# Decode attention and gated MLP on one core: V loads on GpSimd's queue, K loads on SyncE's

## The chip, the cores and the metric

The kernel runs on one core of one Trainium2 chip. The time is device microseconds of one execution; three runs of the kernel before gave 1279.21, 1279.48 and 1279.5 us, median 1279.48 us. Lower is better.

## The reference

One decode step of a transformer layer: layer norm, attention over a cached K and V, a residual, a second layer norm and a sigmoid-gated MLP with a residual. Batch B is 4, one query position, model width 512, 32 heads of 128, a cache of 8192 positions, MLP width 1792, all in bf16.

```python
def _A_ref(x, k_cache, v_cache, wq, wo):
    q = (x @ wq).reshape(B, Sq, H, Dh).transpose(0, 2, 1, 3)
    scores = einsum("bhqd,bhkd->bhqk", q, k_cache) * Dh ** -0.5
    o = einsum("bhqk,bhkd->bhqd", softmax(scores, axis=-1), v_cache)
    return o.transpose(0, 2, 1, 3).reshape(B, Sq, H * Dh) @ wo
def _B_ref(x, w_gate, w_up, w_down):
    return (sigmoid(x @ w_gate) * (x @ w_up)) @ w_down
h  = x + _A_ref(layernorm(x), k_cache, v_cache, wq, wo)
h2 = h + _B_ref(layernorm(h), w_gate, w_up, w_down)
```

k_cache and v_cache have 4 x 32 x 8192 x 128 values each, 268 MB apiece; the weights together are about 14 MB.

## The kernel before

**Units and slots.** The work is cut into NU = 32 units of HU = 4 heads each. The K of a unit, and its V, is one load of 128 partitions x 64 KB, 8 MB. SBUF has three such slots in the tile KV: K alternates between slots 0 and 1, V always uses slot 2, except the last V, which goes to slot 0. Slot 2 first holds wq, so V of unit 0 waits until the q projection (L300, token `t_qp`) has read it. After the last unit, wo, w_gate and w_up go to slot 1 and w_down to slot 2.

**One unit** (`unit`, L421). `scores(u)`: 16 chunks; for each, VectorE transposes 128 x 1024 words of K into one of two halves of kT (L334) and TensorE multiplies it with q in four matmuls (L343). `maxima(u)`: a small memset on VectorE (L360) gives the token `t_kd[u]`, "K of unit u has been read", then come the maximum (L361 to L366) and the exponential on ScalarE (L368). Then `pv(u - 1)`, the product with V of the unit before: 64 matmuls on TensorE (L404), which wait for the load of V, a scaled copy on ScalarE (L409), and a gathering matmul (L414), of which the first one gives `t_vd[u-1]`, "V of unit u-1 has been read". Then `weights(u)`: VectorE transposes the exponentials (L374), and TensorE sums them (L378). L374 waits for the L414 matmuls of the unit before, since the tile PTz is used again. The three compute engines run these in program order; each engine has its own list of instructions, and `_Prog` puts in the waits.

**Loads.** All big loads stand on SyncE's queue in one written order (`order`, L224; issued at L540): k0, k1, v0, k2, v1, k3, and so on to k31, v30, v31. K of unit u waits for `t_kd[u-2]`, V of unit u for `t_vd[u-1]`, the last V for `t_kd[30]`. SyncE issues in order, so a load whose wait is over still stands behind the one ahead of it. Then come 40 empty instructions, and wo (L545), w_gate (L547), w_up (L551), which wait for `t_kd[31]`, and w_down in three pieces (L556), which wait for `t_vd[30]`.

**Semaphores.** A load counts 16 on the semaphore of its slot: k0, k1 and v2 belong to one waiting engine each ("private"), which counts them down again in its loop (`_rebase`); the last V counts on v0.

**The end.** After the last unit TensorE runs filler matmuls (L387) and the last product with V, then the output projection (L474), the layer norm, the gated MLP (L491 to L520) and the output.

**GpSimd** makes masks, identities and zeros in the first 8 us and then does nothing.

Of the kernel before, what the change touches and what calls it, by code (L numbers as in the profile page):

```python
# [18 lines left out]
class _Prog:  # L19
# [52 lines left out]
    def emit(self, eng, fn, waits=(), incs=1, ch=None):  # L72
        todo = self._waits(eng, waits)
        key = ch or eng
        tok = self.token(key, incs) if incs else None
        self._put(eng, todo, key, fn, incs, 1)
        return tok
# [41 lines left out]
def bass_sequential_preLN__mha_block_cached__glu_gated_glu__decode_kernel(  # L119
# [20 lines left out]
    NU = B * H // HU  # L140
    R = S // 32
    SLOT = R * DH
# [11 lines left out]
    prog = _Prog({"p2d": "dve", "d2d": "dve", "a2d": "dve", "d2p": "pe", "a2p": "pe",  # L154
                  "d2a": "act", "p2a": "act",
                  "k0": "dve", "k1": "dve", "v2": "pe"})
    emit = prog.emit

    with ExitStack() as es:
# [39 lines left out]
        def reg(slot, off, size):  # L199
            return KV[:, slot * SLOT + off:slot * SLOT + off + size]  # L200
# [14 lines left out]
        bank = [PS[:, 512 * i:512 * (i + 1)] for i in range(8)]  # L215
        SBK, OBK, EX, XS, XO, QB, DN = 0, 1, 2, 3, 4, (5, 6), 7

        keys = ["sp", "act", "dve", "pool", "pe", "p2x", "d2x", "x", "pad", "out0", "wq", "wg", "v0", "v1"]
        keys += [f"wd{i}" for i in range(len(WDT) - 1)] + [f"wu{i}" for i in range(len(WUC) - 1)] + ["wo"]
        keys += list(prog.private)  # L220
        for k in keys:
            prog.sems[k] = es.enter_context(nc.semaphore("s_" + k))

        order = [("k", 0)] + [x for u in range(1, NU) for x in (("k", u), ("v", u - 1))] + [("v", NU - 1)]  # L224
        slots = {(x, u): (0 if u == NU - 1 else 2) if x == "v" else u % 2 for x, u in order}
        toks = {x: prog.token(x[0] + str(slots[x]), 16) for x in order}
        t_wq = prog.token("wq", 16)
        t_wo = prog.token("wo", 16)
        t_wg = prog.token("wg", 16)
# [64 lines left out]
        for g in range(2):  # L294
# [8 lines left out]
            t_qp = emit("pe", f, [t_wq, t_xn, t_ps0, t_selc], incs=4)  # L303

            src = bank[QB[g]].rearrange("p (k w r) -> p r k w", k=8, r=2)
# [6 lines left out]
        t_tr, t_sc, t_pv, t_ex, t_mx, t_exp, t_ptz, t_lq, t_ocp, t_rs, t_kd, t_vd, t_sum = ({} for _ in range(13))  # L312
# [125 lines left out]
        for u in range(1, NU):  # L438
            t, first = divmod(u - 1, TU)
            if u == NU - 1:  # L440
                prog.close("dve", "act")
                t = 0
# [81 lines left out]
        for t in range(NFT):  # L524
            if t == 0:
# [4 lines left out]

        prog.dma("sp", "wq", lambda e: e.dma_start(reg(2, 0, NC * H * DH), A_wq.rearrange("(p c) f -> p (c f)", p=128)),
                 tok=t_wq)
        for n, (x, u) in enumerate(order):
            w = t_qp if n == 2 else None
            if n >= 3:
                w = t_kd[u - 2] if x == "k" else t_kd[NU - 2] if u == NU - 1 else t_vd[u - 1]
            slot = slots[x, u]
            cache = A_v_cache if x == "v" else A_k_cache
            src = cache[u // (NU // B), HU * (u % (NU // B)):HU * (u % (NU // B) + 1), :, :].rearrange("h (p r) d -> (h p) (r d)", p=32)
            prog.dma("sp", f"{x}{slot}", lambda e, src=src, slot=slot: e.dma_start(reg(slot, 0, SLOT), src), [w],  # L540
                     tok=toks[x, u])
        for _ in range(40):
            emit("sp", lambda e: e.nop(), ch="pad")
        k_done, v_done = t_kd[NU - 1], t_vd[NU - 2]
# [46 lines left out]
```

## Time and profile before

| | |
|---|---|
| time, median of three runs | 1279.48 us |
| lowest and highest | 1279.21 and 1279.5 us |
| span of the profiled execution, first to last instruction | 1277.7 us |
| TensorE matmul busy | 797.8 us (62%) |
| TensorE weight load busy | 327.1 us (26%) |
| VectorE busy | 763.3 us (60%) |
| ScalarE busy | 58.9 us (5%) |
| GpSimd busy | 5.7 us |
| moved by the DMA engines | 550.83 MB, mean 431 GB/s |
| mean granted TensorE clock | 0.822 |

The profiled execution has no time listed apart from its span; the runs listed beside it are some 1.8 us longer than the span, which starts at the first and ends at the last instruction.

How to read it: the span is cut into 40 slices of 31.9 us for the rows of busy tenths. In the groups and the timeline, a row is line, engine, operation, output<-input and count; in the timeline the first two numbers are the start and the length in us, and the bracket at the end is how long the engine had been idle and what released it. In the list of waits the three numbers are the us in total, the times and the longest. In the table of stretches each engine has its busy us and count, followed by the granted clock, the busy share of the 16 DMA engines and GB/s. Queue rows of the DMA part are packets, MB and the share of 16 engines' time. Rows of DMA issues end with the median us from issue to landing. SPq is SyncE's queue, ACTq ScalarE's.

### The profile page before, as it was taken

What the parts mean: (1) busy time and instruction counts of PE and PEld (TensorE: products, weight loads), DVE (VectorE), ACT (ScalarE), POOL (GpSimd) and SP (SyncE); (2) the same over time, 40 slices, a digit from 0 to 9 for tenths busy, and PEclk for the clock granted to TensorE, in tenths of its full rate; (3) what the DMA queues carried; (4) which work ended last, traced back from release to release, by engine and by line L of the source; (5) the groups of instructions that cost most, each with busy time, mean ns of one, the idle gap of its engine ahead of it and who ended that gap; (6) DMA issues with size and microseconds to landing.
All of it is one profiled execution on the core that took longest, in us unless ns stands there. A gap on an engine that the chain in (4) does not pass through costs nothing. (4 is left out here: it accounts for less than half of the span.)

```text
span 1277.7 us, 14121 instructions
## 1 busy us (share of the span) xinstructions
PE 797.8 (62%) x4636; PEld 327.1 (26%) x4636; DVE 763.3 (60%) x917; ACT 58.9 (5%) x114; POOL 5.7 (0%) x22
## 2 busy tenths in 40 slices
PE   1676765557755557655567655567555576555578
PEld 0232222222222223222222222222222232222233
DVE  1876665556665557665567655566655566655571
ACT  2000000000000000000000000000000000000001
POOL 1000000000000000000000000000000000000000
PEclk9988877788877788877788777788777888777888
DMA  9999999999999999999999999999999999999998
GB/s 427 427 425 429 427 455 427 431 427 435 447 427 431 427 437 445 427 431 427 445 437 429 429 427 451 431 429 429 427 453 429 429 429 427 455 427 429 429 429 368
DMA packets 10244, 550.83 MB, mean 431 GB/s; under 512 B 1144, under 2 KB 1152, under 8 KB 1408
## 3 DMA queue, kind: packets, MB, share of 16 engines
q1 hardware_dynamic: 10224, 550.77, 99.7%
q8 instruction: 2, 0.03, 0.0%
q14 instruction: 2, 0.02, 0.0%
q10 hardware_dynamic: 16, 0.01, 0.0%
HBM read 550.77 MB, written 0.00 MB: 431 GB/s over the span
## 5 line engine op out<-in xcount | busy, mean ns | idle before, releaser
L334 DVE STREAM_TRANSPOSE kT<-KV 128x1024 f32<-128x1024 f32 x512 | 615.1, 1233 | 301.1 <-DMA KV<-in_A_k_cache_dram 241.0
L343 PE MATMUL PS<-kT,Lq 128*128 128x512 bf16 x2048 | 586.1, 417 | 320.2 <-DVE kT L334 302.6
L343 PEld LDWEIGHTS PS<-kT,Lq 128*128 x2048 | 209.6, 102 | 697.0 <-issue 623.6
L374 DVE STREAM_TRANSPOSE PTz<-E_sb 32x512 bf16<-32x512 bf16 x128 | 89.9, 703 | 128.9 <-PE PS L414 125.2
L404 PE MATMUL PS<-KV,PTz 128*16 128x512 bf16 x2048 | 116.9, 381 | 0.0
L378 PE MATMUL PS<-part,headw 128*128 128x2 f32 x64 | 18.7, 362 | 100.5 <-DVE PTz L374 100.5
L368 ACT ACTIVATE E_sb<-PS,negm 128x512 bf16<-128x512 f32 x32 | 22.0, 687 | 1141.2 <-DVE negm L366 1141.2
L404 PEld LDWEIGHTS PS<-KV,PTz 128*16 128x16 bf16 x2048 | 58.3, 109 | 56.8 <-issue 13.2
L414 PE MATMUL PS<-lane,kT 128*128 128x4 f32 x256 | 33.6, 255 | 30.9 <-ACT kT L409 30.9
L361 DVE TENSOR_REDUCE part<-PS 128x1 f32<-128x512 f32 x32 | 22.1, 692 | 38.8 <-PE PS L343 38.8
L414 PEld LDWEIGHTS PS<-lane,kT 128*128 128x128 f32 x256 | 31.0, 191 | 46.3 <-issue 44.9
L378 PEld LDWEIGHTS PS<-part,headw 128*128 128x128 f32 x64 | 16.0, 310 | 103.7 <-DVE PTz L374 103.7
L321 PE MATMUL PS<-Lq,headw 128*128 128x512 bf16 x32 | 18.7, 585 | 10.9 <-issue 9.5
L409 ACT ACTIVATE kT<-PS,rsb 128x512 f32<-128x512 f32 x32 | 22.0, 687 | 61.1 <-PE PS L404 61.1
L387 PE MATMUL PS<-Lq 128*128 128x512 bf16 x44 | 13.7, 478 | 0.2 <-issue 0.2
L327 DVE TENSOR_TENSOR Lq<-q_all,mask 128x32 bf16<-128x32 bf16 x32 | 9.7, 303 | 0.0
L453 DVE TENSOR_TENSOR kT<-PS,mask 128x512 bf16<-128x512 f32 x1 | 0.7, 692 | 12.9 <-PE PS L414 12.9
L366 DVE STREAM_TRANSPOSE negm<-mxr 128x32 f32<-128x32 f32 x32 | 6.8, 212 | 1.1
L363 DVE STREAM_TRANSPOSE turn<-part 128x32 f32<-128x32 f32 x32 | 6.8, 212 | 1.1
L387 PEld LDWEIGHTS PS<-Lq 128*128 128x128 bf16 x44 | 4.8, 115 | 8.2 <-issue 5.8
L395 DVE RECIPROCAL rsb<-PS 128x1 f32<-128x1 f32 x32 | 6.5, 202 | 0.7 <-PE PS L378 0.7
L300 PE MATMUL PS<-KV,kT 128*4 128x512 bf16 x32 | 3.6, 627 | 5.1 <-DMA KV<-in_A_wq_dram 5.1
(70 smaller groups left out, 59.5 us busy)
## 6 DMA issues: line engine op xcount, KB each, us to landing
KV<-in_A_wq_dram SPq DMA_DIRECT2D x1, 4096.0 KB, 12.2
KV<-in_A_wo_dram SPq DMA_DIRECT2D x1, 4096.0 KB, 27.5
KV<-in_B_w_gate_dram SPq DMA_DIRECT2D x1, 1792.0 KB, 31.4
KV<-in_B_w_up_dram SPq DMA_DIRECT2D x1, 1792.0 KB, 35.2
KV<-in_B_w_down_dram SPq DMA_DIRECT2D x1, 1024.0 KB, 32.5
KV<-in_A_k_cache_dram SPq DMA_DIRECT2D x32, 49.8
KV<-in_A_v_cache_dram SPq DMA_DIRECT2D x32, 30.8
KV<-in_B_w_down_dram SPq DMA_DIRECT2D x1, 512.0 KB, 33.3
```

The lines of the kernel that those rows point to most:

```text
L321: emit("pe", lambda e: e.matmul(bank[bk], headb, zeros, start=True, stop=False, skip_group_check=True), waits, incs=0)
L327: t_lq[u] = emit("dve", lambda e, ix: e.tensor_tensor(dst, bass.AP(raw(q_all), at(ix, 0) * (4 * TU) + 4 * (u - TU * t), [[NU * 4, 128], [1 ...
L334: t_tr[u, c] = emit("dve", lambda e: e.transpose(kT[:, (c % 2) * TW:(c % 2 + 1) * TW], KVw[:, o:o + TW]), w, ch="d2p")
L343: ins = e.matmul(bank[SBK], bass.AP(raw(Lq), ix[-1] * 2 + (128 * t + c % 2), [[528, 128], [1, 128]]), rhs, start=False, stop=False, skip_g ...
L361: a = emit("dve", lambda e: e.tensor_reduce(part[:, 0:1], bank[SBK], AX.X, ALU.max), [t_sc[u, NT - 1], t_pool], ch="d2d")
L368: t_exp[u] = emit("act", lambda e: e.activation(E_sb[:, :], bank[SBK], ACT.Exp, bias=negm[:, 0:1], scale=SCALE, accum_out=part[:, 1:2]), [ ...
L374: return [e.transpose(PTz[32 * q:32 * (q + 1), :].rearrange("p (r q c) -> p r q c", r=4, q=4)[:, :, q, :], E_sb[32 * q:32 * (q + 1), :].re ...
L378: t_sum[u] = emit("pe", lambda e: e.matmul(bank[QB[1]][:, 0:2], headw[:, :], part[:, 0:2], start=True, stop=True), [t_ptz[u], t_selc], ch= ...
L387: emit("pe", lambda e: [e.matmul(bank[XS], Lq[:, 0:128], Lq[:, 0:512], start=True, stop=True) for _ in range(n)][-1], [t_ps0, t_lq[NU - 1] ...
L404: made.append(e.matmul(PS[32 * j:32 * j + 16, ob:ob + 512], lhsT, KV[:, slot * SLOT + 512 * k:slot * SLOT + 512 * (k + 1)], start=(k < 4), ...
L409: t_ocp[u] = emit("act", lambda e: e.activation(O_sb, bank[OBK], ACT.Copy, scale=rsb[:, 0:1]), [t_pv[u], t_rs[u]], ch="a2p")
L414: ins = e.matmul(bass.AP(raw(PS), at(ix, 0) * 4 + (512 * EX + 4 * (u - t)), [[4096, 128], [1, 4]]), O_sb[:, 128 * q:128 * (q + 1)], lane[: ...
```

## The change

V of units 0 to 28 is issued from GpSimd instead of SyncE, each with the same wait as before. Such a load counts on a new semaphore `vs`; GpSimd waits for it and then adds 16 to v2, on which TensorE waits, with an empty instruction. SyncE issues K of all 32 units, each with the same wait as before, then V of unit 29, the first half (by columns) of the last V, V of unit 30, and the second half of the last V; then the 40 empty instructions and the weights as before. The last V counts 32 on v0, for both halves. Slots and sizes are the same; the compute engines' code is not touched.

```diff
-        keys = ["sp", "act", "dve", "pool", "pe", "p2x", "d2x", "x", "pad", "out0", "wq", "wg", "v0", "v1"]
+        keys = ["sp", "act", "dve", "pool", "pe", "p2x", "d2x", "x", "pad", "vs", "out0", "wq", "wg", "v0", "v1"]
...
-        order = [("k", 0)] + [x for u in range(1, NU) for x in (("k", u), ("v", u - 1))] + [("v", NU - 1)]
+        order = [(x, u) for u in range(NU) for x in "kv"]
         slots = {(x, u): (0 if u == NU - 1 else 2) if x == "v" else u % 2 for x, u in order}
-        toks = {x: prog.token(x[0] + str(slots[x]), 16) for x in order}
+        toks = {x: prog.token(x[0] + str(slots[x]), 16 + 16 * (x == ("v", NU - 1))) for x in order}
+        APART = NU - 3
...
-        for n, (x, u) in enumerate(order):
-            w = t_qp if n == 2 else None
-            if n >= 3:
-                w = t_kd[u - 2] if x == "k" else t_kd[NU - 2] if u == NU - 1 else t_vd[u - 1]
+        def load(eng, x, u, w, a=0, b=SLOT):
             slot = slots[x, u]
             cache = A_v_cache if x == "v" else A_k_cache
             src = cache[...]
-            prog.dma("sp", f"{x}{slot}", lambda e, src=src, slot=slot: e.dma_start(reg(slot, 0, SLOT), src), [w],
-                     tok=toks[x, u])
+            if eng == "pool":
+                t = prog.dma(eng, "vs", lambda e: e.dma_start(reg(slot, a, b - a), src[:, a:b]), [w])
+                prog.dma(eng, f"{x}{slot}", lambda e: e.nop(), [t], tok=toks[x, u])
+            else:
+                prog.dma(eng, f"{x}{slot}", lambda e: e.dma_start(reg(slot, a, b - a), src[:, a:b]), [w], tok=toks[x, u])
+
+        for u in range(NU):
+            load("sp", "k", u, t_kd[u - 2] if u > 1 else None)
+        for u in range(APART):
+            load("pool", "v", u, t_vd[u - 1] if u else t_qp)
+        load("sp", "v", NU - 3, t_vd[NU - 4])
+        load("sp", "v", NU - 1, t_kd[NU - 2], 0, SLOT // 2)
+        load("sp", "v", NU - 2, t_vd[NU - 3])
+        load("sp", "v", NU - 1, t_kd[NU - 2], SLOT // 2)
```

## The prediction

> **What bounds the kernel now.** I read the page's queue table first, then the stretches of the span, then what SyncE's queue waited for, then single transfers in the timeline.
>
> ```profile
> span 1277.7 us, 14121 instructions
> PE 797.8 (62%) x4636; PEld 327.1 (26%) x4636; DVE 763.3 (60%) x917; ACT 58.9 (5%) x114; POOL 5.7 (0%) x22
> q1 hardware_dynamic: 10224, 550.77, 99.7%
> 90.60:1235.00 1144.40, 717.69 (x4094) 295.01 (x4094) 702.86 (x830) 42.48 (x87) 0.00 (x0) 0.81 1.00 433
> SPq L540 <- PE PS L414: 1124.4, 30, 38.5
> DVE kT L334 <- DMA KV<-in_A_k_cache_dram: 241.0, 31, 14.3
> ```
>
> No compute engine is busy for more than 62% of the span. The one queue that carries all bulk data, q1 (SyncE's), keeps the 16 DMA engines at work for 99.7% of it, and in the 1144 us stretch without start and end the DMA share is 1.00. The queue still waits 1124.4 us for L414, the matmul that frees V's only slot. That wait costs nothing, because a K load is always in flight beneath it. VectorE idles 241.0 us for K. So the bound is the sum of bytes: what the change can save is DMA idle time, of which 0.3% of 1277.7 = 3.8 us exist, and what it can cost is any moment in which no queue holds a load.
>
> The time of one load (8 MB, K or V), and the rest of the unit's schedule:
>
> ```profile
> 1175.23 2.37 DVE L334 STREAM_TRANSPOSE kT<-KV 128x1024 f32<-128x1024 f32 x2 [7.30 <-DMA KV<-in_A_k_cache_dram]
> 1196.48 0.06 DVE L360 MEMSET dumm<- 128x1 f32 x1
> 1197.64 3.65 PE L404 MATMUL PS<-KV,PTz 128*16 128x512 bf16 x64
> 1202.68 0.80 SPq L540 DMA_DIRECT2D KV<-in_A_v_cache_dram  x2
> 1203.42 2.90 DVE L374 STREAM_TRANSPOSE PTz<-E_sb 32x512 bf16<-32x512 bf16 x4 [4.04 <-PE PS L414]
> 1213.92 2.37 DVE L334 STREAM_TRANSPOSE kT<-KV 128x1024 f32<-128x1024 f32 x2 [7.60 <-DMA KV<-in_A_k_cache_dram]
> ```
>
> The first and last of these are the arrivals of K30 and K31 with one V between them: 38.69 us for two loads, **19.35 us per load**. K30 is scored (L334 transposes, L343 matmuls) from 1175.23 to the marker L360 at 1196.48, 21.2 us. TensorE starts the V product 1.16 us after that marker; 5.04 us after its start the V slot is free (the L540 issue at 1202.68), and 8.68 us after its start VectorE has finished the L374 transposes (1203.42 + 2.90) and can start the next K.
>
> The listed runs have a median of 1279.48 us; the span is 1277.7, so about 1.8 us lie around it. I make the sum against 1279.5. Less than 0.2% (2.6 us) would hardly be told from no change here.
>
> **The change, part by part.** *Removed:* SyncE's fixed order V(u), K(u+2). Before, both go out together when the V slot comes free, and are served one after the other. *Added:* V of units 0 to 28 on GpSimd's queue, and a semaphore step by GpSimd behind each. K(u+2) now leaves as soon as unit u is scored, some 6.2 us sooner (1202.68 less 1196.48). The bytes are the same, so nothing is gained while a load is always in flight.
>
> How two queues with bulk loads share the DMA engines is not in this trace. Its nearest rows are the small instruction queues in a stretch where q1 is full:
>
> ```profile
> q1 hardware_dynamic: 236, 13.50, 104.2%
> q8 instruction: 1, 0.02, 0.2%
> q14 instruction: 1, 0.01, 0.1%
> ```
>
> They got their packets in 60 to 90 us although SyncE's queue had a load in flight all the while and mostly another behind it. The share of V has the ends 0 (K first while both wait) and 1 (V first). I take one half, because a K row and a V row have the same 64 KB (8192 KB over 128 partitions), and other queues do get in between. The Trainium skill, page "DMA: Bandwidth & Descriptors", section "Queues, rings and completion order", says each DMA engine takes turns between queues, one packet at a time, and that a packet can hold many descriptors. The rows agree with turns; how much of a load one turn moves they do not show, and rival C has the other extreme.
>
> *Start-up.* The rows:
>
> ```profile
> 0.80 0.56 ACTq L234 DMA_DIRECT2D KV<-in_A_x_dram  x1
> 2.86 0.68 DVE L272 BATCH_NORM_STATS2 kT<-KV 4x6 f32<-4x512 bf16 x1 [2.86 <-DMA KV<-in_A_x_dram]
> 13.01 3.58 PE L300 MATMUL PS<-KV,kT 128*4 128x512 bf16 x32 [5.06 <-DMA KV<-in_A_wq_dram]
> 1.23 0.89 SPq L540 DMA_DIRECT2D KV<-in_A_k_cache_dram  x2
> 16.71 0.33 SPq L540 DMA_DIRECT2D KV<-in_A_v_cache_dram  x1
> 32.32 2.37 DVE L334 STREAM_TRANSPOSE kT<-KV 128x1024 f32<-128x1024 f32 x2 [14.25 <-DMA KV<-in_A_k_cache_dram]
> 53.34 0.06 DVE L360 MEMSET dumm<- 128x1 f32 x1
> 59.80 2.37 DVE L334 STREAM_TRANSPOSE kT<-KV 128x1024 f32<-128x1024 f32 x2
> 80.82 0.06 DVE L360 MEMSET dumm<- 128x1 f32 x1
> ```
>
> wq lands at 13.0, then K0 moves, landing at 32.3. V0 is issued at 16.7. The 4 KB x load took 2.06 us from issue (0.80) to its reader (2.86); for the time from issue to first bytes I take 1.5 us, with 0.5 to 4 as ends, since no load from GpSimd is in this trace. Before, V0 queued behind K0 and K1. Now it starts at 18.2 beside K0, which has 5.2 of its 19.35 us done; the other 14.1 go at half speed, 28.3 us, so **K0 lands at 46.5 instead of 32.3**. Scoring with K at hand takes 21.0 us (32.32 to 53.34, and 59.80 to 80.82), and 6.46 us lie between the first unit's marker and the next transposes (53.34 to 59.80). So unit 0 is scored at 67.5, when K2 goes out, and unit 1 from 74.0 (K1 is there at 13.0 + 3 x 19.35 = 71.1) to 95.0, when K3 goes out, with first bytes at 96.5. V1 waits for the product of unit 0, later still (95.0 + 6.2). All that can move until then is K0, K1, V0 and K2: 13.0 + 4 x 19.35 = 90.4. **From 90.4 to 96.5 the DMA engines have nothing: 6.1 us lost.** Counted by whole rows (8 of 2.42 us per load and engine, K0's third finished before V's first) K0 lands at 44 to 45 and the loss is 4 to 4.5. A later V0 shortens it, as K0 then moves alone for longer (at 4 us, 3.6). I take 5.5, range 3 to 7. Before, the V0 behind K1 filled just this gap.
>
> *Steady state.* Call L the landing of a V. GpSimd's step adds a hop; the nearest row is a GpSimd instruction that waits for the one ahead of it:
>
> ```profile
> 1.17 0.20 POOL L237 TENSOR_SCALAR_AFFINE_SELECT ident<-ident 128x16 bf16<-128x16 bf16 x1 [0.23 <-POOL ident L236]
> ```
>
> It idled 0.23 us; I take 0.3 (0.1 to 1). Queued behind that wait on GpSimd is only the next V load, which has to wait for TensorE's product anyway. On TensorE, behind the wait for V, stand L414, L378 and the next unit's L343, and VectorE's L374 waits for them. So the product starts at L+0.3, the next V is issued at L+5.3 with first bytes at L+6.8, VectorE is free at L+9.0, the next unit is scored at L+30.1, and its K (two units ahead) has first bytes at L+31.6. Now unit 1: K3 leaves 6.2 us before V1, so it has 6.2 done and 13.15 to share; V1 and the rest run at half speed for 38.7 us, by when K4 (issued 30.9 after K3, still under K3's tail) has 6.2 done. Then L: K4 alone for 6.8, 6.35 left; V2 shares for 12.7 and gets 6.35, is alone from L+19.5 to L+31.6 for 12.1, and has 0.9 left when K5 arrives. It lands at L+33.4. K5 has 0.9 + 6.8 done, 11.65 left, lands 30.1 after that V; V3 has 11.65 + 1.5 by K6's first bytes, 6.2 left, and lands at 44.0, with K6 at 6.2: where the round began. Two units take 33.4 + 44.0 = 77.4 = 4 x 19.35, **no idle, but a margin of only 0.9 us** in each second unit. Each microsecond by which V is faster or compute later than this, beyond 0.9, opens a DMA gap in some 14 pairs of units. I put 1 us, ends 0 and 14.
>
> *The end.* With V29, both halves of V31 and V30 on SyncE's queue behind K31, there is one queue again. The first half of V31 (9.7 us) waits only for unit 30's scores and covers the 6.8 us in which V30 waits for the slot; without that cover 6.8 us would be lost. The rest keeps its order:
>
> ```profile
> 1235.04 0.33 SPq L545 DMA_DIRECT2D KV<-in_A_wo_dram  x1
> 1252.92 3.17 PEld L404 LDWEIGHTS PS<-KV,PTz 128*16 128x16 bf16 x64 [0.42 <-DMA KV<-in_A_v_cache_dram]
> 1241.51 33.33 DMA KV<-in_B_w_down_dram
> ```
>
> The product of V31 waited on its load at 1252.92, and the last w_down piece, issued at 1241.14 and landing at 1274.84, ends the chain. V31's second half lands just ahead of wo as V31 did, so the tail moves as a whole: 0.
>
> **Sum:** 1279.5 + 5.5 + 1 = **1286.0 us**; own range 1281 to 1300.
>
> **Rivals.**
> A. *Served in order of issue.* If V0 does not get in ahead of K1's queued rows, K0 lands at 32.3, K1 at 51.7, V0 at 71, as before, no gap arises at the start, and later K is just queued sooner: 1279.5, not slower. It decides at one point, K0's landing. For it: K0 and K1 are issued 15 us ahead of V0 (1.23 against 16.71). Against it: the instruction queues' packets. Chance 0.10.
> B. *V starts some 3 us later* because GpSimd is held up by VectorE when it issues: L374's 2.90 us stand right there. At start-up K0 lands at 43.6 and the gap is 3.2; in the pairs K has 17.5 of its load done when V begins, V shares only 3.7 us, is alone for 18.2 and done 0.7 us before K's first bytes: 14 x 0.7 = 10. 1279.5 + 3.2 + 10 = 1292.7. The Trainium skill, page "SBUF — State Buffer", section "SBUF: two separate sides", says descriptors of a GpSimd DMA cannot be written while VectorE runs a two-port operation; whether these transposes are such, no row here shows. Chance 0.10.
> C. *Turns of whole loads.* V0 then moves from 18.2 ahead of K0's rest, K0 lands at 51.7, unit 0 is scored at 72.7 (K2's first bytes 74.2, while K1 was done at 71.0: 3.2 lost), unit 1 at 100.2; K2 is done at 93.5, K3 begins at 101.7: 8.2 lost. 1279.5 + 11.4 = 1290.9, more where V is always first, up to some 1318. Chance 0.08.
> D. *V starved*, if its pieces are smaller and K goes first. Then V lands at L, the next at L+26.2 with 6.8 us idle before it and 5.4 after it until K at L+31.6; K to 51.0, V till the next K at 62.5, K to 81.9, V's rest 7.8: 89.7 for two units instead of 77.4, 14 x 12.3 = 172: some 1450, and 1300 to 1450 for shares between. Against it: same shapes, one instruction per load as now. Chance 0.10.
> E. *Faster.* Only the 3.8 us of idle and the gaps between rows could go: not below 1275.7; no step that does it. Chance 0.04.
>
> **How the numbers follow.** Forecast 0.58, A 0.10, B 0.10, C 0.08, D 0.10, E 0.04. Faster is E, 0.04; the same is A, 0.10; slower is the rest, 0.86. The range runs from 1278.5 (A) to 1306, through the forecast, B and the lower half of C; D, E and C's upper half stay out.
>
> **What would show it.**
>
> ```profile
> KV<-in_A_k_cache_dram SPq DMA_DIRECT2D x32, 49.8
> KV<-in_A_v_cache_dram SPq DMA_DIRECT2D x32, 30.8
> ```
>
> Those are the medians from issue to landing before. K0's first L334 transposes near 45 instead of 32.3; a hole in the DMA row in the slice around 90 us; K loads landing 33 us after issue, V loads 28 and 39 in turn, against 49.8 and 30.8, GpSimd's issues 33 and 44 us apart; the DMA share 1.00 between. Wrong if K0 still lands at 32 (A), if holes recur every 77 us (B), if V lands under 22 us after issue at the start (C), or if the units take 45 us (D).

## The result, and the profile after

The change makes the kernel slower: **1334.72 us** (median of four runs, 1333.31 to 1335.2) against 1279.35 us before, a ratio of 1.0433 with a 95% interval of 1.0421 to 1.0445. The forecast was 1286.0 us with a range of 1278.5 to 1306: the sign was right, the size far off. The profiled execution took 1333.31 us, its span is 1332.1 us, 54.4 us more than before.

First the page after, head and queues (columns as before; helper lines have moved by one, so L405 is the product with V that was L404, L375 the old L374, L415 the old L414):

```profile
span 1332.1 us, 14103 instructions
DMA  9989999899999989989999998999999899899996
GB/s 409 441 377 425 421 384 441 378 441 441 399 419 409 439 380 441 441 382 437 409 431 419 410 441 378 441 409 427 423 409 439 380 441 441 378 441 409 419 427 264
q1 hardware_dynamic: 6192, 307.50, 54.2%
q0 software_dynamic: 4176, 243.27, 42.2%
```

The DMA row is no longer all nines. The dips to 378 and 380 GB/s come back every two or three slices, 80 us apart. Both queues together hold the engines for 96.4% of a longer span. Three stretches, DMA share and GB/s last:

```profile
89.00:94.00 5.00, 4.29 (x20) 1.69 (x24) 3.71 (x5) 0.00 (x0) 0.00 (x0) 1.00 0.48 157
334.20:336.20 2.00, 1.72 (x8) 0.77 (x8) 1.19 (x2) 0.00 (x0) 0.00 (x0) 1.00 0.00 0
1320.00:1332.10 12.10, 8.58 (x103) 3.36 (x92) 3.87 (x10) 3.77 (x7) 0.00 (x0) 1.00 0.02 6
```

The first is the hole at the start, the second one of those that recur (nothing moves at all), the third the end: 12.1 us of compute in which the DMA engines are all but idle, where 4.1 us stood before (from 1273.6 to the end). Adding up the records of single DMA packets, idle time and busy time each as a mean over the 16 engines, gives this:

```
hole at the start (from 89.7 on), idle                          4.2 us
holes about 80 us apart, 173.1 to 1216.8, 14 of 1.9 to 2.8 us,
  and a small one of 0.6 us at 152.6, idle                     31.4
end, idle beyond what stood there before (11.8 against 3.7)     8.1
packets busy for longer in total (1284.8 against 1274.1)       10.7
together the 54.4 us
```

The longer packets belong to the holes: of the rows that took over 2.48 us, those that start within 4.5 us of the beginning of a hole hold most of the excess; a row that starts on idle engines mostly took 2.9 to 3.4 us instead of 2.42. A recurring hole thus costs some 2.2 us of idle time and 0.6 to 0.7 us of longer rows.

The list of waits shows who waits in place of whom:

```profile
PE PS L405 <- POOLq L540: 235.0, 14, 17.9
DVE PTz L375 <- PE PS L415: 399.6, 31, 24.7
DVE kT L335 <- DMA KV<-in_A_k_cache_dram: 26.3, 1, 26.3
```

Before, VectorE waited 241.0 us for K, 31 times. Now it does so once (K0), and TensorE waits for V, 14 or 15 times, once in two units; VectorE's L375 waits behind it. The cycle in the timeline:

```profile
303.81 5.91 PE L405 MATMUL PS<-KV,PTz 128*16 128x512 bf16 x64 [16.55 <-POOLq L540]
311.37 0.53 POOL L539 DMA_DIRECT2D KV<-in_A_v_cache_dram  x1 [49.33 <-PE PS L415]
335.33 0.06 DVE L361 MEMSET dumm<- 128x1 f32 x1
336.49 3.66 PE L405 MATMUL PS<-KV,PTz 128*16 128x512 bf16 x64
341.80 0.53 POOL L539 DMA_DIRECT2D KV<-in_A_v_cache_dram  x1 [29.89 <-PE PS L415]
365.91 0.06 DVE L361 MEMSET dumm<- 128x1 f32 x1
384.05 5.05 PE L405 MATMUL PS<-KV,PTz 128*16 128x512 bf16 x64 [16.90 <-POOLq L540]
390.75 0.53 POOL L539 DMA_DIRECT2D KV<-in_A_v_cache_dram  x1 [48.43 <-PE PS L415]
```

V6 goes out at 311.37, V7 at 341.80 (30.4 us later), V8 at 390.75 (49.0 later); from pair to pair the short step is 30.4 or 31.2 us and the long one 49.9 or 49.0. In the short step V is there when its product's turn comes (336.49, 1.16 us after the marker). In the long step unit 8 is scored at 365.91, but the product of V7 waits 16.9 us, to 384.05. From V2 to V28 the pairs last 80.2 us each:

```profile
150.52 0.53 POOL L539 DMA_DIRECT2D KV<-in_A_v_cache_dram  x1 [50.87 <-PE PS L415]
1192.80 0.53 POOL L539 DMA_DIRECT2D KV<-in_A_v_cache_dram  x1 [48.39 <-PE PS L415]
```

1042.28 us for 13 pairs, against 77.4 us that four loads need. That is the loss: 2.8 us in each pair.

### The profile page after: what moved, and what is told of

It is laid out like the page before. It is cut to its first block, busy times and chain, and to the rows that moved or that the text cites. A ratio compares the mean times of both kernels' runs of the same rounds, so it can differ in the third digit from the quotient of the medians.

```text
span 1332.1 us, 14103 instructions
## 1 busy us (share of the span) xinstructions
PE 801.6 (60%) x4588; PEld 330.5 (25%) x4636; DVE 762.5 (57%) x917; ACT 59.0 (4%) x114; POOL 21.2 (2%) x51
## 5 line engine op out<-in xcount | busy, mean ns | idle before, releaser
L335 DVE STREAM_TRANSPOSE kT<-KV 128x1024 f32<-128x1024 f32 x512 | 614.6, 1231 | 83.5 <-PE PS L344 42.4
L375 DVE STREAM_TRANSPOSE PTz<-E_sb 32x512 bf16<-32x512 bf16 x128 | 89.9, 703 | 403.3 <-PE PS L415 399.6
L405 PE MATMUL PS<-KV,PTz 128*16 128x512 bf16 x2048 | 145.8, 448 | 244.1 <-POOLq L540 235.0
L405 PEld LDWEIGHTS PS<-KV,PTz 128*16 128x16 bf16 x2048 | 62.0, 117 | 327.1 <-POOLq L540 242.0
L415 PE MATMUL PS<-lane,kT 128*128 128x4 f32 x256 | 33.6, 255 | 31.0 <-ACT kT L410 31.0
L415 PEld LDWEIGHTS PS<-lane,kT 128*128 128x128 f32 x256 | 31.0, 191 | 46.3 <-issue 45.0
L539 POOL DMA_DIRECT2D KV<-in_A_v_cache_dram x29 | 15.5, 533 | 1170.4 <-PE PS L415 1160.8
L388 PE MATMUL PS<-Lq 128*128 128x512 bf16 x27 | 10.8, 455 | 2.8 <-issue 2.2
L322 PEld LDWEIGHTS PS<-Lq,headw 128*128 128x128 bf16 x32 | 3.4, 107 | 13.0 <-issue 11.5
```

Of the source, the lines that this page charges most:

```text
L335: t_tr[u, c] = emit("dve", lambda e: e.transpose(kT[:, (c % 2) * TW:(c % 2 + 1) * TW], KVw[:, o:o + TW]), w, ch="d2p")
L375: return [e.transpose(PTz[32 * q:32 * (q + 1), :].rearrange("p (r q c) -> p r q c", r=4, q=4)[:, :, q, :], E_sb[32 * q:32 * (q + 1), :].re ...
L388: emit("pe", lambda e: [e.matmul(bank[XS], Lq[:, 0:128], Lq[:, 0:512], start=True, stop=True) for _ in range(n)][-1], [t_ps0, t_lq[NU - 1] ...
L405: made.append(e.matmul(PS[32 * j:32 * j + 16, ob:ob + 512], lhsT, KV[:, slot * SLOT + 512 * k:slot * SLOT + 512 * (k + 1)], start=(k < 4), ...
L415: ins = e.matmul(bass.AP(raw(PS), at(ix, 0) * 4 + (512 * EX + 4 * (u - t)), [[4096, 128], [1, 4]]), O_sb[:, 128 * q:128 * (q + 1)], lane[: ...
L539: t = prog.dma(eng, "vs", lambda e: e.dma_start(reg(slot, a, b - a), src[:, a:b]), [w])
```

## The experiments

Two theories stood against each other after the result. *Sharing:* two bulk queues take turns on the DMA engines, and a V load that shares all its way is the longest link of a pair. *Path:* a load issued by GpSimd, or its relay, is slow in itself.

**V from ScalarE's queue (v_act).**

```diff
-        for u in range(APART):
-            load("pool", "v", u, t_vd[u - 1] if u else t_qp)
...
+            prog.dma("act", "v2", lambda e: e.dma_start(reg(2, 0, SLOT), src), [w], tok=toks["v", u])
```

The cut lines put this issue behind the product of each unit on ScalarE, whose instructions are written out here instead of looped.

> V of units 0 to 28 goes out from ScalarE's queue instead of GpSimd's, under the same waits; its landing is told to TensorE directly, without GpSimd's step. Theory (two queues share the DMA engines row by row, and what the sharing costs does not depend on who issues): holes near 2 us in every second unit stay, 1320 to 1332 us, the relay's 0.3 us per pair at most gone. Rival (the GpSimd path is what costs: writing its descriptors, its step): the holes go, 1280 to 1290 us.

1332.89 us, ratio 1.0416 (1.0399 to 1.0433), just above the 1332 that the first theory allowed and far from the rival. The same cycle without GpSimd; the wait stands on the DMA itself:

```profile
303.71 5.16 PE L405 MATMUL PS<-KV,PTz 128*16 128x512 bf16 x64 [16.74 <-DMA KV<-in_A_v_cache_dram]
310.26 0.33 ACTq L437 DMA_DIRECT2D KV<-in_A_v_cache_dram  x1
341.52 0.33 ACTq L437 DMA_DIRECT2D KV<-in_A_v_cache_dram  x1
383.91 6.01 PE L405 MATMUL PS<-KV,PTz 128*16 128x512 bf16 x64 [16.36 <-DMA KV<-in_A_v_cache_dram]
```

42.4 us from V7's issue to its product, against 42.25 with GpSimd. The relay is worth nothing here, and the loss does not depend on who issues.

**All K and V from GpSimd's queue, in the order of before (all_pool).** Issues and relays of both kinds stand in one list on GpSimd:

```diff
+            load("v", u)
+            if u + 2 < NU:
+                load("k", u + 2)
...
+            tell("k", u + 1)
+            tell("v", u)
```

> All K and V from GpSimd's queue, in the order of the kernel before, each told on by a GpSimd step; wq and the weights at the end stay on SyncE's queue. One queue for the bulk loads again, but the GpSimd path for each of 64 loads. Theory (sharing costs): 1279 to 1284 us, no holes. Rival (the GpSimd path costs, about 2 us for each V): 64 loads pay, 1330 us or more.

1284.95 us, ratio 1.0045 (1.0029 to 1.0062): no holes, but 5.9 us more than before, a little over the expectation. All of it lies at the end: the product of V31 waits for its load until 1260.44, where it began at 1252.92 before. There the weights, on SyncE's queue, share with V31.

```profile
1235.53 0.33 SPq L564 DMA_DIRECT2D KV<-in_A_wo_dram  x1
1260.44 5.18 PE L404 MATMUL PS<-KV,PTz 128*16 128x512 bf16 x64 [7.10 <-POOLq L544]
```

**The weights on GpSimd's queue too (all_pool_w).** The same, with `prog.dma("pool", ...)` for wo, w_gate, w_up and w_down.

> All K and V and the weights at the end from GpSimd's queue, in the order of the kernel before; only wq stays on SyncE's. The run with K and V alone on GpSimd's queue took 5.9 us more than before, all of it after the last DMA. Theory (there the weights on SyncE's queue shared the engines with the last V and made its product late): the 5.9 us go, 1279 to 1281 us. Rival (GpSimd's path makes the end late): 1284 to 1286 us.

1279.25 us, ratio 1.0006 (0.9996 to 1.0015), and the product of V31 begins at 1252.80. So 70 bulk loads through GpSimd cost nothing that can be measured, as long as they are the only queue. The path theory is out.

**The order of the change on one queue (one_queue).**

```diff
+        for u in range(1, NU - 2):
+            load("sp", "k", u + 2, t_kd[u])
+            load("sp", "v", u, t_vd[u - 1])
```

> The change without GpSimd: all loads on SyncE's queue, K of unit u+2 ahead of V of unit u, so K still leaves as soon as its slot is free; the end as in the change (K31, V29, first half of V31, V30, second half). Theory: no holes in the middle, since nothing is shared; what is left is the longer end of the change, some 8 us: 1285 to 1290 us. Rival (the earlier K is what hurts, V coming late): 1320 us or more.

1287.92 us, ratio 1.0072 (1.0055 to 1.0089), as expected: the earlier K does no harm in the middle, and the end costs what it costs in the change (11.4 us in which next to nothing is moved):

```profile
300.00:400.00 100.00, 67.73 (x338) 25.96 (x336) 64.94 (x78) 3.71 (x8) 0.00 (x0) 0.88 1.01 436
1275.30:1286.70 11.40, 7.86 (x88) 3.07 (x80) 3.88 (x10) 3.78 (x7) 0.00 (x0) 1.00 0.01 3
```

**V of unit 0 behind K1 on SyncE's queue (v0_sp).**

```diff
+            if u == 1:
+                load("sp", "v", 0, t_qp)
```

> The change, but V of unit 0 on SyncE's queue behind K1, so that it does not slow K0. The 4 us hole near 90 us goes in every theory. Theory (the pairs of units carry on whatever lead K and V had at the start, and a lead that is larger keeps the holes away or under 0.5 us): 1284 to 1296 us. Rival (each V pays a fixed price on its way, whatever the lead): only the 4 us go, 1328 to 1332 us.

1323.41 us, ratio 1.0342 (1.0324 to 1.0359): between the two expectations, and the reason behind mine fell. The hole at the start is gone (DMA share 0.97 in 89 to 94 us), and the first of the recurring holes comes at 205.8 instead of 152.6; but then the pairs settle at the same length, with holes of the same 2.1 to 2.5 us:

```profile
293.63 0.53 POOL L539 DMA_DIRECT2D KV<-in_A_v_cache_dram  x1 [30.74 <-PE PS L415]
1176.10 0.53 POOL L539 DMA_DIRECT2D KV<-in_A_v_cache_dram  x1 [29.93 <-PE PS L415]
```

882.47 us for 11 pairs, 80.2 us. No lead is carried on: the pair is a chain that is longer than its bytes.

**Both halved, and K alone halved (halves, k_halves).** Rows of 32 KB on both queues keep the shares and halve the turns; rows of 32 KB for K alone give V two thirds.

```diff
+                for c in range(a, b, SLOT // 2):
+                    prog.dma(eng, f"{x}{slot}", lambda e, c=c: e.dma_start(reg(slot, c, SLOT // 2), src[:, c:c + SLOT // 2]), [w],
+                             tok=toks[x, u])
```

> The change, but K and the V of units 0 to 28 each in two loads of half the columns: all rows 32 KB, shares equal again, a turn half as long. Theory A (the shared link as a whole, 38.7 us of DMA time at half speed, sets the pair; the turns only cut it at its ends): about as the change, 1325 to 1337 us. Theory B (the turns do it: two rows' wait at V's start, one row's wait of its completion behind K, 7.3 us in all, halved to 3.6): the pair falls under the 77.4 us that the bytes need, the holes go, 1292 to 1300 us.

> The change, but each K in two loads of half its columns, so a K row is 32 KB and a V row 64 KB: beside each other V gets two thirds. Theory (a V load that has to share all its way is the longest link of each pair of units, 34 us of rows and 7 us around them): its rows take 29 us, the link is no longer the longest and the recurring holes go; at the start V0 takes more from K0, which lands at 51 to 52 instead of 44, and the holes there grow to 3.4 and 8.2 us; with the end's 8 us some 1295 to 1303 us. Rival (two queues at once cost something whatever the shares, 2 us a pair): 1335 us or more.

1333.04 us with both halved, ratio 1.0418 (1.0401 to 1.0436), as theory A has it; 1303.74 us with K halved, ratio 1.0195 (1.0178 to 1.0212), just above the 1303 expected. What counts is V's share, not the length of a turn. With two thirds the recurring holes are gone; the two at the start grow (3.5 and 7.3 us of idle time by the packet records, where 3.4 and 8.2 were expected):

```profile
300.00:400.00 100.00, 68.66 (x384) 27.26 (x377) 61.15 (x70) 3.62 (x7) 1.58 (x3) 0.84 1.01 436
70.00:75.00 5.00, 3.39 (x14) 1.16 (x12) 3.67 (x6) 0.00 (x0) 0.00 (x0) 1.00 0.37 105
93.00:102.00 9.00, 7.85 (x44) 3.03 (x48) 7.52 (x8) 0.00 (x0) 0.00 (x0) 1.00 0.22 69
```

**V halved (v_halves),** one third for V.

```diff
+                prog.dma(eng, "vs", lambda e: e.dma_start(reg(slot, 0, m), src[:, 0:m]), [w])
+                t = prog.dma(eng, "vs", lambda e: e.dma_start(reg(slot, m, m), src[:, m:2 * m]))
```

> The change, but each V of units 0 to 28 in two loads of half its columns, K whole: beside each other V gets one third. Theory (V's shared load is the longest link of a pair): it lengthens by up to half its time, holes in nearly every unit, 1400 to 1440 us. Rival (no dependence on shares): 1332 us.

1436.39 us (two runs), ratio 1.123 (1.1208 to 1.1253), as expected, and holes in nearly every unit:

```profile
GB/s 409 447 410 434 288 414 367 372 440 305 438 354 376 438 321 426 362 369 391 355 434 365 367 378 371 436 332 424 351 380 438 307 438 365 392 411 321 424 426 268
```

With one third, a half and two thirds the time falls from 1436 over 1335 to 1304.

**TensorE kept busy in the wait (warm, warm_long).** 36, then 74 matmuls of zeros ahead of the waiting product; what is computed for the output stays the same.

```diff
+            emit("pe", lambda e: [e.matmul(bank[XS], headb, zeros, start=True, stop=True) for _ in range(n)][-1], incs=0)
```

> The change, with 36 matmuls of zeros on TensorE in every second unit, ahead of the product that waits 17 us for its V, so that the product runs on a TensorE that has not been idle (it took 5 to 6.2 us after the wait, 3.65 elsewhere); TensorE's loop body is two units for this. They write a spare bank and fill some 15.5 us of the wait. Theory (the pair is a chain: scoring, a shared V load, that product): up to 2 us less per pair over 14 pairs, 1302 to 1315 us. Rival (only the loads matter, the product is hidden): 1330 to 1336 us.

1332.92 us, ratio 1.042 (1.0403 to 1.0438), in the rival's range, but inconclusive: the 36 took 8.00 us, not 15.5, TensorE idled again for 8.7 us, and the product still took 5.0 to 6.3 us.

```profile
367.68 8.00 PE L425 MATMUL PS<-Lq,headw 128*128 128x512 bf16 x36
384.39 5.92 PE L405 MATMUL PS<-KV,PTz 128*16 128x512 bf16 x64 [8.72 <-POOLq L551]
```

> As the run with 36 matmuls, but 74: the 36 filled only 8 of the 17 us of the wait (0.22 us each, not 0.43), and the product behind them still took 5.2 to 5.9 us, so the question stayed open. 74 of them fill 16.4 us. Theory (chain): the product at 3.7 to 4 us, up to 2 us less per pair over 14 pairs, 1302 to 1320 us. Rival (start of a V falls on K's row boundaries and swallows such gains, or the product is hidden): 1328 to 1336 us.

1316.92 us, ratio 1.0296 (1.0278 to 1.0313), as expected. The product is down to 3.66 us and the pair to 78.7 us (V5's issue at 260.19, V9's at 417.61: 157.42 us for two):

```profile
364.42 16.27 PE L425 MATMUL PS<-Lq,headw 128*128 128x512 bf16 x74
380.80 3.66 PE L405 MATMUL PS<-KV,PTz 128*16 128x512 bf16 x64
260.19 0.53 POOL L550 DMA_DIRECT2D KV<-in_A_v_cache_dram  x1 [31.26 <-PE PS L415]
417.61 0.53 POOL L550 DMA_DIRECT2D KV<-in_A_v_cache_dram  x1 [30.98 <-PE PS L415]
```

1.5 us less in each pair, 17.8 us in all. The product after the wait is a link of the chain.

**A plain end (plain_end).** V29, V30 and an undivided V31.

```diff
-        load("sp", "v", NU - 1, t_kd[NU - 2], 0, SLOT // 2)
         load("sp", "v", NU - 2, t_vd[NU - 3])
-        load("sp", "v", NU - 1, t_kd[NU - 2], SLOT // 2)
+        load("sp", "v", NU - 1, t_kd[NU - 2])
```

> The change, but with the last three V on SyncE's queue in plain order, V29, V30, V31, the last one whole. Theory (the first half of V31 ahead of V30 makes V30 and with it the last scoring late, so the end is compute): some 5 to 9 us less, 1325 to 1330 us. Rival (the end is late because V29 already is): the same as the change, 1332 to 1336 us.

1334.97 us, ratio 1.0436 (1.0419 to 1.0454): no change, my theory of the end fell. The cover did what the prediction says of it: without it the DMA engines are nearly idle from 1258.1 to 1267.9. Yet the product of V31 begins at 1308.59, as in the change (1308.66), so the compute up to it did not hang on that cover. The loads that follow are later, though: here the last chain runs over a piece of w_down, which lands at 1331.08, and TensorE waits 0.7 us for w_up and 1.1 us for w_down. In this run compute and loads end almost together.

```profile
1258.10:1267.90 9.80, 7.30 (x72) 3.19 (x72) 0.67 (x1) 0.69 (x1) 0.00 (x0) 0.67 0.23 80
1308.59 3.65 PE L405 MATMUL PS<-KV,PTz 128*16 128x512 bf16 x64
1297.45 33.63 DMA KV<-in_B_w_down_dram
```

**K halved and V0 behind K1 (k_halves_v0).** Both edits above together.

> K in half rows, and V of unit 0 on SyncE's queue behind K1. Theory (the start's holes come from V0 taking from K0, the recurring ones from V's half share, the end from V29 behind K31): the start's 10.6 us of holes in the run with K in halves go, nothing recurs, the end's 8 us stay: 1286 to 1293 us. Rival (V0 early also sets the lead on which the later pairs run): holes come back, 1300 us or more.

1290.77 us, ratio 1.0093 (1.0076 to 1.011): as expected. The start and the pairs are mended, the end is left.

**The same without the 24 filler matmuls ahead of the last product (short_end).**

```diff
-        filler(2, 12)
```

> The run with K in half rows and V of unit 0 on SyncE's queue, without the 24 filler matmuls ahead of the last product (7 us on TensorE; they compute nothing that is used). Theory (the end is a chain of compute from V29's product on, 73 us): 5 to 7 us less, 1284 to 1286 us. Rival (the end waits for V31 or for the weights): no change, 1290 to 1292 us, the product waiting for its load instead.

1285.23 us, ratio 1.0042 (1.0028 to 1.0056), 5.5 us less. The last product moves from 1266.18 to 1258.84 and, without fillers, takes 6.20 us instead of 3.65. So the end is a chain of compute in these kernels. In three kernels with the end of the change it has the same length from V29's product on: 1332.1 - 1258.88 = 73.2 us in the change, 1286.7 - 1214.12 = 72.6 in one_queue, 1289.6 - 1216.78 = 72.8 in k_halves_v0. Before it was 1277.7 - 1197.64 = 80.1, with 7 us of slack behind loads.

```profile
1258.88 6.23 PE L405 MATMUL PS<-KV,PTz 128*16 128x512 bf16 x64 [9.09 <-DMA KV<-in_A_v_cache_dram]
1214.12 5.89 PE L405 MATMUL PS<-KV,PTz 128*16 128x512 bf16 x64 [5.12 <-DMA KV<-in_A_v_cache_dram]
1216.78 6.06 PE L405 MATMUL PS<-KV,PTz 128*16 128x512 bf16 x64 [4.56 <-DMA KV<-in_A_v_cache_dram]
1258.84 6.20 PE L405 MATMUL PS<-KV,PTz 128*16 128x512 bf16 x64
```

The lines are the product of V29 in the change, in one_queue and in k_halves_v0, and the last product in short_end. No version here beats the kernel before; all_pool_w equals it.

## Why the prediction was right and wrong

**Right: the bound, the share, the start.** The DMA engines did set the time before (99.7% busy), and V's share is one half where both queues hold a load: one row of the one queue, then one of the other. K0 landed at 44.42 (forecast by whole rows 44 to 45), so rival A is out; unit 0 was scored at 65.32, unit 1 at 92.66:

```profile
44.42 2.37 DVE L335 STREAM_TRANSPOSE kT<-KV 128x1024 f32<-128x1024 f32 x2 [26.34 <-DMA KV<-in_A_k_cache_dram]
92.66 0.06 DVE L361 MEMSET dumm<- 128x1 f32 x1
```

The hole behind them is 4.2 us (4 to 4.5 by rows, 5.5 taken). That the landing fits so well is in part luck. V0's first row came at 21.8, 4.8 us after its issue, so four rows of K0 and not three moved alone; and K0's completion came only after one more row of V0. The two errors of 2.4 us cancel. They are the two ends of a shared load on which the steady state went wrong.

The Trainium skill, page "DMA: Bandwidth & Descriptors", section "Queues, rings and completion order", says engines take turns packet by packet. The trace agrees, and settles the size here: one 64 KB row a turn, so rival C is out. The Trainium skill, page "SBUF — State Buffer", section "SBUF: two separate sides", would have GpSimd's loads held up while VectorE runs an operation that takes the port pair they share. No run here shows that: V from ScalarE's queue ran the same cycle, and all_pool_w had no loss with the issues of V and K right at L374's transposes. So the cause that rival B names is out. Its effect came: V did start some 3 us late and holes did recur, which was B's sign, but because V waits its turn behind K, and at 2.8 us a pair where B had 0.7. D's place was right for another share: at one third the time is 1436.

**Wrong: the steady state, one term of the sum.** I closed a pair at exactly 77.4 us, with 0.9 us to spare, and priced a shortfall at 1 us in all. The step that failed is the long one of each pair, in which V shares its whole way: 44.0 us in my sum, 49.0 in the trace. It was mis-sized in four places. V7 in the change, beside the prediction's V3: from issue to its first row 4.9 us instead of 1.5; its rows 34.3 us instead of 37.2; from the last row to the product 3.05 us instead of 0.3; from there to the next issue 6.70 us instead of 5.04. That is 48.95 instead of 44.0. The short step cannot make up for it, since it stands on compute: 30.4 us (21 us of scoring, the product and the transposes) is its floor, 3.0 under the 33.4 that I gave it. 30.4 + 49.0 is longer than 77.4, and what is longer is a hole.

The first row: after the issue at 341.80 only SyncE's queue starts rows until 346.5, two for each engine, then V's first ones come. And the landing: V's last rows end at 381.0, but its completions, packets of 4 bytes, come after one more row of K. From the DMA view in narrow windows (packets, MB):

```profile
q1 hardware_dynamic: 32, 2.10, 103.2%
q0 software_dynamic: 16, 1.05, 96.8%
q0 software_dynamic: 16, 0.00, 0.8%
```

The windows are 341.8 to 346.5 (that row alone: no V), 346.5 to 349, and 382.8 to 384: 16 packets of 0.00 MB, the completions. These two ends of a shared load I had left out, and the product on a TensorE that had idled 17 us I had priced at its length elsewhere. They are the same in every long step: 4.8 to 5.0 us to the first row, and 2.4 us from the last row to the completions. Of these terms only the product was taken away by itself (1.5 us a pair); the first two are read from the trace, not isolated. The run with both halved shows that shorter turns alone do not help: its V7 is issued at 340.43, has its first rows 3.6 to 5.0 us later and its product 1.8 us after its last row, but its 16 half rows have 14 half rows of K between them, where the 8 whole rows had 6 of K; so they take some 36 us, and V8 is again issued 49.0 us after V7. I had also named only a faster V, or later compute, as what opens gaps; here it was a V that lands later in the long step.

Also wrong was that a margin, once there, is carried on, which V0 behind K1 shows. And my likeliest value put the recurring loss at the low end of the bounds that I had written down, 0 to 14; it was 14 pairs x 2.8 = 39 us, outside them. The sum had 5.5 + 1 + 0; the runs have some 5 at the start, some 41 in the pairs (the small hole at 152.6 included) and 8 at the end.

**Wrong: the end.** I put the tail at 0, as the order of the last loads was kept and each gap covered. But V29 and K31 had changed places. The price was 8 us: the product of V29, which now stands behind K31 in one queue, waits 9.09 us for its load, and from there the end is 73 us of compute that loads no longer cover. Whether V29 ahead of K31 would win these 8 us was not tried. I had checked which load comes last, not which chain.

## What to carry to other kernels

Here a second queue for bulk loads brought no bandwidth, since one already kept the DMA engines busy for 99.7% of the span; it changed which load is served when, and a V that the next step needs soon took 42 us from issue to product beside a K that is needed late, where a load alone needs 19.35. Before splitting a stream, lay out one whole cycle with every link: the row that is under way, the completion, the engine that has gone idle; and compare the longest chain with the bytes. A margin of 0.9 us in a cycle of 77.4 was no margin, and the range has to reach past the point where it is gone.

## What was not expected of the hardware

Beside another bulk queue V7's first row came 4.9 us after its issue from GpSimd's queue and 5.1 us after it from ScalarE's, two rows of the other queue (2.42 us each) in between, and its completion 2.4 us after its last row, one row of the other queue. A row that starts on idle DMA engines mostly took 2.9 to 3.4 us. A product of 64 matmuls took 3.65 us in the flow; in the change it took 5.0 to 6.3 us after TensorE had waited 9 to 18 us, and over all runs 4.9 to 6.6 us after 4 us and more. GpSimd's bulk loads, alone on their queue, were as fast as SyncE's: ratio 1.0006 (0.9996 to 1.0015).
